# Middle stages of a spectral filter as 64x64 float32 blocks in four quarters of the TensorE array

## Chip, cores and metric

The kernel runs on 1 core of one Trainium2 chip. The metric is the time of one execution on the device in microseconds. Three runs of the kernel before took 3160.31, 3162.1 and 3166.95 us; the median is 3162.1 us.

## What is computed

```python
# x: (8, 3072, 256), filt: (1537, 256) complex
X = rfft(x, axis=1);  y = irfft(X * (filt_r + 1j * filt_i))      # spectral filter
xk = mu_k * y + (1 - mu_k) * y_prev;  xr = mu_r * y + (1 - mu_r) * y_prev   # y_prev: one token back
k = maximum(xk @ w_k, 0);  v = (k * k) @ w_v                     # 256 -> 1024 -> 256
z = sigmoid(xr @ w_r) * v
h = maximum(maximum(z @ w1, z @ w2), z @ w3)                     # 256 -> 768
out = h @ w_out                                                  # 768 -> 256
```

All inputs and outputs are float32.

## The kernel before

A sequence of 3072 tokens is transformed as 96 x 32 points. Stage A works over the 96, and its result goes to DRAM (`s1a`, `s1b`) as 24 groups of four rows for each of 32 residues, 128 rows x 256 channels for a group. Stage B is a 128x128 matrix for each group; its output is multiplied by the complex filter; stage C is another 128x128 matrix for each group, and its result goes to DRAM (`s2`). `y_load` and `y_mm` read it back by chunks of 384 tokens and do the last stage of the inverse transform. B and C are the middle stages. Batch 0 has a transform of its own at the start (`fft_first`). The seven others are done by `fft(b + 1)` beside the dense layers of batch `b`.

In `fft`, B and C go by steps of two groups: 12 steps a batch, 84 in all. Each product is three matmuls in fp32r: high weights by high data, high by low, low by high (`mm3`, L227). So `b_mm` (L489) and `c_mm` (L506) are six matmuls of 128x128 by 256 columns each, into one PSUM bank. For this `split` (L249) makes two parts of the data: a cast on ScalarE (L250) and a subtraction on GpSimd (L251). `b_load` (L476) brings the four weight parts of two groups (512 KB, from a copy in DRAM, `wbc_d`, that twelve GpSimd DMAs make early in the kernel, L1011), the filter (512 KB) and the data (256 KB), and splits the data. After the matmuls of B, three VectorE instructions (L497 to L499) read the bank and multiply by the filter, GpSimd adds (L500), and the sum is split again. After those of C, ScalarE copies the bank (L512) and issues the store.

The order: the dense layers are a list of small units with weights (`units`), the transform of the next batch a list of pieces with weights (`pieces`), and `drive` (L180) mixes them in proportion. A piece of B or C weighs 0.65; an empty piece of 6.0 stands between the first load of B and its first use. That gives the emission order. Each engine's final order is made by a scheduler, which follows a simulated time line and takes of the instructions that are ready the one emitted first, unless it is told another priority. Every matmul waits in TensorE's one queue. All PSUM tiles come from one pool of eight banks under one tag (`ps`, tag `pm`). The SBUF pool `fp` has tags with two or three buffers: `filt`, `fhi`, `flo` and `wbc` three, `fin` and `fo` two. An instruction that needs a buffer waits until the last reader of the buffer's earlier tile is done.

float32 matmuls occur in `fft_first`, in `y_mm` and in `wu_job`; the trace shows each as two records, each with a weight load of its own.

Of the kernel before, what the change touches and what calls it, by code (L numbers as in the profile page):

```python
# [16 lines left out]
N = 3072  # L17
N1 = 48
# [9 lines left out]
GB = NG - GA  # L28
ORDER = [g for g in range(NG) if g % NR == 0] + [g for g in range(NG) if g % NR]


def fft_constants():
# [5 lines left out]
    wi = np.zeros((2, 2, NG, NP))  # L38
    for j in range(2):
        for g in range(NG):  # L40
            ph = 2 * np.pi * ((n1 * g) % N1) / N1
            if g == 0:
                wa[j::2, 0, j, 0] = 1.0
                wa[j::2, 1, j, 0] = (-1.0) ** n1
                wi[0, j, 0, j::2] = 1.0 / N
                wi[1, j, 0, j::2] = (-1.0) ** n1 / N
            else:
                wa[j::2, 0, j, g] = np.cos(ph)
                wa[j::2, 1, j, g] = -np.sin(ph)
                wi[0, j, g, j::2] = 2 * np.cos(ph) / N  # L50
                wi[1, j, g, j::2] = -2 * np.sin(ph) / N
    wb = np.zeros((2, N2, NG, 2, N2))
    wc = np.zeros((2, N2, NG, 2, N2))
    freq = np.zeros((2, N2, NG), np.int64)
    for g in range(NG):
        for s in range(N2):
            if g:
# [8 lines left out]
                wc[0, s, g, 0, :] = c  # L66
                wc[1, s, g, 0, :] = -sg * sn
                wc[0, s, g, 1, :] = sn
                wc[1, s, g, 1, :] = sg * c
                freq[:, s, g] = f if s < NM else N - f  # L70
            else:
# [5 lines left out]
                if s == 0:  # L77
                    wb[0, :, 0, 0, 0] = 1.0
                    wb[0, :, 0, 1, 0] = (-1.0) ** n2
                    wc[0, 0, 0, 0, :] = 1.0  # L80
                    wc[1, 0, 0, 0, :] = (-1.0) ** n2
                    freq[1, 0, 0] = N // 2
                else:
                    wb[src, :, 0, 0, s] = c
                    wb[src, :, 0, 1, s] = -sn
                    wc[0, s, 0, src, :] = 2 * c
                    wc[1, s, 0, src, :] = -2 * sn

    wa, wi, wb, wc, freq = wa[..., ORDER], wi[:, :, ORDER], wb[:, :, ORDER], wc[:, :, ORDER], freq[:, :, ORDER]
    wb = wb.reshape(4, NM, NG, NK).transpose(1, 0, 2, 3)  # L90
    wc = wc.reshape(NK, NG, 4, NM).transpose(0, 1, 3, 2)
    return (
        wa.reshape(NP, NQ),
        wi.reshape(NQ, NP),
        wb.reshape(NK, NG, NK),
        wc.reshape(NK, NG, NK),
# [4 lines left out]
def radix3_constants():  # L101
# [31 lines left out]

    m = np.arange(NM)
    wb = np.zeros((NM, 4, NG, 2, N2))
    for a, g in enumerate(ORDER):
        for s in range(N2):
            if g:
# [8 lines left out]
                wb[:, r + 1, a, 1, s] = sg * cj * c  # L147
            elif s == 0:
                wb[:, 0, a, 0, 0] = 1.0
                wb[:, 0, a, 1, 0] = (-1.0) ** m  # L150
            else:
# [3 lines left out]
                if s < NM:  # L155
                    wb[:, s % 2, a, 0, s] = c
                    wb[:, s % 2, a, 1, s] = -sn
                else:
# [5 lines left out]
    return w3, wb.reshape(NK, NG, NK)  # L164
# [33 lines left out]
def tile_spectral_moe(ctx: ExitStack, tc, x, xr, xz, filt, ones, wa, wa1, wi, wbc, wb1, wc1, filt1, filt0, mu, w_k, w_v, w_r, w1, w2, w3, w_out, out):  # L198
# [25 lines left out]
    def mm(o, wgt, rhs, start, stop, more=False):  # L224
        nc.tensor.matmul(o, lhsT=wgt, rhs=rhs, start=start, stop=stop, skip_group_check=more)  # L225
# [15 lines left out]
    mu_s = cpool.tile([P, 2, 2], F32, name="mu_s")  # L241
    nmu_s = cpool.tile([P, 2, 2], F32, name="nmu_s")
# [839 lines left out]
```

## Time and profile before

| | |
|---|---|
| median of three runs | 3162.1 us |
| profiled execution | 3161.27 us |
| its span, first to last instruction | 3159.5 us |
| TensorE matmuls busy | 3080.0 us, 97%, 19172 records |
| TensorE weight loads busy | 3020.4 us, 96% |
| VectorE / ScalarE / GpSimd busy | 1922.4 / 1884.8 / 1858.6 us (61 / 60 / 59%) |
| mean granted TensorE clock | 0.990 |
| DMA | 705.92 MB, mean 223 GB/s |

A record of a matmul lasts longer than the distance to the next one, since the array is pipelined: the busy time says whether TensorE had a matmul under way, and the distance between two starts says what one costs.

### The profile page before, as it was taken

The page shows a single profiled execution, that of the slowest core. Times are in us where ns is not written, and L with a number is a line of the kernel's source. Part 1 is how long each engine was busy: PE and PEld are TensorE (multiplying, and loading weights), DVE is VectorE, ACT ScalarE, POOL GpSimd, SP SyncE. Part 2 cuts the span into 40 slices and gives each one's busy share as a digit, 9 for nine tenths or more (in the row PEclk, how much of TensorE's full clock was granted, in tenths as well). Part 3 has the DMA queues.
Part 4 walks back from the last instruction along what each step waited for, and adds up shares of the span by engine and source line. Part 5 has one row for each costly group of instructions (what it writes and reads, how often), then busy time and mean ns, then how long its engine had stood idle before and what let it go on. Part 6 is the DMA issues. An engine that isn't in the chain of part 4 may idle for free.

```text
span 3159.5 us, 55818 instructions
## 1 busy us (share of the span) xinstructions
PE 3080.0 (97%) x19172; PEld 3020.4 (96%) x19172; DVE 1922.4 (61%) x3050; ACT 1884.8 (60%) x3968; POOL 1858.6 (59%) x1591
## 2 busy tenths in 40 slices
PE   6799999999999999999999999999999999999998
PEld 4699999999999999999999999999999999999998
DVE  4976676556664666556655566656666566555554
ACT  5556656566565566656666556566666566555554
POOL 3545765567554676556756566556765468444443
PEclk8899999999999999999999999999999999999999
DMA  9878787667776677758767587765887567555554
GB/s 298 267 260 285 235 305 227 188 197 251 260 233 184 224 240 227 254 171 259 251 221 220 183 263 261 227 205 183 262 268 237 180 214 232 178 169 165 161 170 122
DMA packets 400951, 705.92 MB, mean 223 GB/s; under 512 B 41472, under 2 KB 153120, under 8 KB 400032
## 3 DMA queue, kind: packets, MB, share of 16 engines
q1 hardware_dynamic: 333648, 621.26, 62.1%
q10 hardware_dynamic: 64576, 72.45, 6.5%
q0 software_dynamic: 2448, 8.65, 0.8%
q8 instruction: 155, 2.54, 0.3%
q14 instruction: 124, 1.02, 0.1%
HBM read 616.35 MB, written 92.14 MB: 224 GB/s over the span
## 4 chain that ended last, share of the span: by engine, by line
PE 81%; DVE 6%; DMA 5%; POOL 3%; issue 3%; ACT 1%; ACTq 0%; SPq 0%; POOLq 0%; DVEq 0%
PE pb L225 17%; PE pk L225 15%; PE pv L225 14%; PE po L225 12%; PE pe L225 8%; PE pa L225 5%; PE pr L225 4%; PE py L225 3%; DMA ws<-wud 3%; PE pc L225 2%; DVE sc L773 1%; POOL klo L251 1%; DMA s<-e 1%; DVE xd L427 1%; POOL hh L251 1%
## 5 line engine op out<-in xcount | busy, mean ns | idle before, releaser
L225 PE MATMUL pb<-x,ws 128*128 128x384 f32 x3456 | 751.7, 337 | 10.2 <-DMA ws<-wud 7.0
L251 POOL TENSOR_TENSOR hh<-m,hh 128x384 fp32r<-128x384 f32 x384 | 409.5, 1075 | 563.5 <-ACT hh L250 481.4
L251 POOL TENSOR_TENSOR klo<-kr,khi 128x384 fp32r<-128x384 f32 x492 | 520.8, 1064 | 233.2 <-ACT khi L250 205.1
L225 PEld LDWEIGHTS pb<-x,ws 128*128 128x128 f32 x3456 | 596.1, 188 | 20.5 <-issue 6.4
L741 DVE SCALAR_TENSOR_TENSOR kr<-pk,kr 128x384 f32<-128x384 f32 x512 | 281.4, 553 | 429.7 <-ACT kr L740 427.5
L225 PE MATMUL pv<-khi,ws 128*128 128x384 f32 x2048 | 481.3, 338 | 4.9 <-ACT khi L250 4.9
L225 PE MATMUL po<-wo_hi,hh 128*128 128x256 f32 x2304 | 481.4, 282 | 3.3 <-ACT hh L250 2.6
L250 ACT CAST khi<-kr 128x384 fp32r<-128x384 f32 x512 | 261.9, 513 | 226.8 <-DVE kr L741 191.9
L225 PEld LDWEIGHTS po<-wo_hi,hh 128*128 128x128 f32 x2304 | 391.1, 189 | 5.0 <-ACT hh L250 3.4
L225 PE MATMUL pe<-x,ws 128*128 128x384 f32 x1728 | 387.8, 338 | 3.5 <-DVE m L848 1.4
L225 PEld LDWEIGHTS pv<-khi,ws 128*128 128x128 f32 x2048 | 358.9, 188 | 8.5 <-ACT khi L250 6.4
L225 PE MATMUL pk<-xh,wk_hi 128*128 128x384 f32 x1024 | 341.2, 336 | 3.8 <-ACT xh L250 3.8
L225 PE MATMUL pk<-xl,wk_hi 128*128 128x384 f32 x1024 | 343.7, 336 | 0.9 <-DVE xl L251 0.9
L225 PE MATMUL pk<-xh,wk_lo 128*128 128x384 f32 x1024 | 343.3, 335 | 0.0
L225 PE MATMUL po<-wo_lo,hh 128*128 128x256 f32 x1152 | 316.8, 282 | 0.0
L740 ACT ACTIVATE kr<-pk 128x384 f32<-128x384 f32 x512 | 249.8, 489 | 108.8 <-POOL klo L251 56.8
L225 PEld LDWEIGHTS pe<-x,ws 128*128 128x128 f32 x1728 | 297.4, 188 | 8.8 <-DVE sc L855 3.1
L225 PE MATMUL pv<-klo,ws 128*128 128x384 f32 x1024 | 298.6, 338 | 2.4 <-DVE klo L251 1.3
L856 DVE TENSOR_TENSOR m<-sc,m 128x384 f32<-128x384 f32 x384 | 293.9, 768 | 8.4
L251 POOL TENSOR_TENSOR xl<-xm,xh 128x768 fp32r<-128x768 f32 x126 | 234.9, 1880 | 70.3 <-ACT xh L250 70.2
L250 ACT CAST hh<-m 128x384 fp32r<-128x384 f32 x384 | 192.6, 514 | 123.5 <-DVE m L856 85.6
L809 ACT COPY v<-pb 128x384 f32<-128x384 f32 x288 | 138.3, 480 | 188.8 <-PE pb L225 181.4
(134 smaller groups left out, 6143.1 us busy)
## 6 DMA issues: line engine op xcount, KB each, us to landing
ws<-wud SPq DMA_DIRECT2D x864, 256.0 KB, 3.8
ws<-wvd SPq DMA_DIRECT2D x512, 256.0 KB, 3.7
wbc<-wbcd SPq DMA_DIRECT2D x84, 512.0 KB, 5.5
filt<-in_filt SPq DMA_DIRECT2D x84, 512.0 KB, 4.3
ws<-wud SPq DMA_DIRECT2D x288, 128.0 KB, 3.7
xz<-in_xz SPq DMA_DIRECT2D x56, 512.0 KB, 5.2
cin<-s SPq DMA_DIRECT2D x64, 384.0 KB, 4.1
out_dram<-osb ACTq DMA_DIRECT2D x192, 128.0 KB, 2.9
```

Source lines behind the costliest of these rows:

```text
L225: nc.tensor.matmul(o, lhsT=wgt, rhs=rhs, start=start, stop=stop, skip_group_check=more)
L250: nc.scalar.copy(hi, src)
L251: (lo_eng or nc.gpsimd).tensor_tensor(lo, src, hi.bitcast(F32), ALU.subtract)
L427: nc.vector.tensor_tensor(v, z[:, 0], z[:, 1], ALU.subtract)
L740: nc.scalar.activation(r, p, AF.Relu)
L741: nc.vector.scalar_tensor_tensor(r, p, 0.0, r, ALU.max, ALU.mult)
L773: eng.tensor_tensor(t, a, b, ALU.subtract)
L809: nc.scalar.copy(st[to], st[of])
L856: nc.vector.tensor_tensor(m, c, m, ALU.max)
```

## The change

Stages B and C become 64x64 blocks. The frequencies of a group are sorted by parity (`halves_of`), so that each 128x128 matrix of a group is two 64x64 blocks. A step now takes four groups (`NU4` = 6 steps a batch). `quarters` issues eight matmuls of 64x64 by 256 columns in float32: for each pair index `k`, one in each quarter of the array, (rows y, columns x). They go into two PSUM banks, one for each half of the array's rows, and are issued inside `tc.high_priority()`, which gives them the priority of the program's start. There are no parts and no splits of data. The product with the filter is made in each half of 64 partitions: ScalarE copies two blocks of 32 partitions with a sign, VectorE has three instructions, GpSimd multiplies 64 partitions and adds 128. Weights are loaded from the input itself, 256 KB for four groups; the DRAM copy and its twelve GpSimd DMAs go. `s2` has another layout, and `y_load` reads it in two DMAs instead of one. The weights of pieces become 1.1 and 7.7.

```diff
-    def mm(o, wgt, rhs, start, stop, more=False):
-        nc.tensor.matmul(o, lhsT=wgt, rhs=rhs, start=start, stop=stop, skip_group_check=more)
+    def mm(o, wgt, rhs, start, stop, more=False, at=None):
+        nc.tensor.matmul(o, lhsT=wgt, rhs=rhs, start=start, stop=stop, skip_group_check=more, tile_position=at)
...
-    wbc_d = [dp.tile([NK, 4, 2, NK], F32R, tag=f"wbcd{s}", name=f"wbcd{s}", bufs=1) for s in range(NG // 2)]
...
-        s2 = dp.tile([NM, 4, NG, C], F32, tag="s2", name=f"s2_{b}")
+        s2 = dp.tile([2, NM, 2, NG, C], F32, tag="s2", name=f"s2_{b}")
...
+        def quarters(o, of):
+
+            for k in range(2):
+                for y in range(2):
+                    for x in range(2):
+                        w, d = of(y, x, k)
+                        with tc.high_priority():
+                            mm(o[y][x * H : x * H + H, k], w, d, k == 0, True, True, (y * H, x * H))
+
+        def b_load(u):
+            w = fp.tile([NK, 2, 2, 2, H], F32, tag="fhi", name="wbc", bufs=3)
+            nc.sync.dma_start(w, wbc[:, u])
+            f = []
+            sv, g = (s1a, 4 * u) if 4 * u < GA else (s1b, 4 * u - GA)
+            t = fp.tile([NK, 4, C], F32, tag="wbc", name="xb", bufs=3)
+            for y in range(2):
+                d = sv[:, 2 * y : 2 * y + 2, g : g + 4].rearrange("m r g c -> m r (g c)")
+                nc.sync.dma_start(t[y * H : y * H + H], d)
+            for z in range(2):
+                f.append(fp.tile([NK, 2, 2, C], F32, tag="filt", name="filt", bufs=3))
+                nc.sync.dma_start(f[z], filt[:, u, z])
+            st["b", u] = w, f, t
+
+        def b_mm(u):
+            w, f, t = st.pop(("b", u))
+            p = [ps.tile([NK, 2, C], F32, tag="pm", name="pb") for _ in range(2)]
+            quarters(p, lambda y, x, k: (w[y * H : y * H + H, 0, x, k], t[y * H : y * H + H, 2 * x + k]))
+            y = []
+            for z in range(2):
+                fr, fi, q = f[z][:, 0], f[z][:, 1], p[z]
+                v = fp.tile([NK, 2, C], F32, tag="flo", name="v", bufs=3)
+                a, e, m = slice(0, NM), slice(NM, H), NM
+                lo, hi = slice(H, H + NM), slice(H + NM, NK)
+                nc.scalar.mul(v[lo], q[hi], sg_s[hi])
+                nc.scalar.mul(v[hi], q[lo], sg_s[lo])
+                nc.vector.scalar_tensor_tensor(fi[a], q[e], -1.0, fi[a], ALU.mult, ALU.mult)
+                nc.vector.tensor_tensor(fi[e], q[a], fi[e], ALU.mult)
+                nc.vector.tensor_tensor(fr, q, fr, ALU.mult)
+                nc.gpsimd.tensor_tensor(fi[H:], v[H:], fi[H:], ALU.mult)
+                yz = fp.tile([NK, 2, C], F32, tag="fin", name="yz")
+                nc.gpsimd.tensor_tensor(yz, fr, fi, ALU.add)
+                y.append(yz)
+            st["c", u] = w, y
+
+        def c_mm(u):
+            w, t = st.pop(("c", u))
+            p = [ps.tile([NK, 2, C], F32, tag="pm", name="pc") for _ in range(2)]
+            quarters(p, lambda y, x, k: (w[y * H : y * H + H, 1, x, k], t[x][y * H : y * H + H, k]))
+            sv = s2.rearrange("h m r g c -> (h m r) g c")
+            for y in range(2):
+                o = fp.tile([NK, 2, C], F32, tag="fo", name="co")
+                nc.scalar.copy(o, p[y])
+                g = 4 * u + 2 * y
+                nc.scalar.dma_start(sv[:, g : g + 2, :], o)
+
+        for u in range(NU4 + 2):
+            def pb(u=u):
+                if u < NU4:
+                    b_load(u)
+                if 1 <= u <= NU4:
+                    b_mm(u - 1)
+            def pc(u=u):
+                if u >= 2:
+                    c_mm(u - 2)
+            pieces.append((1.1, pb))
+            if u == 0:
+
+                pieces.append((7.7, lambda: None))
+            pieces.append((1.1, pc))
...
-        nc.sync.dma_start(t, s2v[:, q * MC : (q + 1) * MC, :])
+        for h in range(2):
+            nc.sync.dma_start(t[h * 2 * NG : (h + 1) * 2 * NG], s2v[h, :, q * MC : (q + 1) * MC, :])
...
-    for s in range(NG // 2):
-        units.insert(20 + 5 * s, (0.0, lambda s=s: tc.keep_in_program_order(nc.gpsimd.dma_start(wbc_d[s], wbc[:, s]))))
-    n2 = len(wjobs2) + NG // 2
+    n2 = len(wjobs2)
```

The constants of the new layout are made on the host in `radix3_constants` and `quarter_layout`, and so are the input arrays `in_wbc`, `in_filt` and `in_wi`; the shapes of `in_wc1` and of the tensors of `fft_first` stay as they are.

## Rows read from the trace of the kernel before

**Rows 1.** The page: span, then busy us, share of the span and instructions by engine

```profile
span 3159.5 us, 55818 instructions
PE 3080.0 (97%) x19172; PEld 3020.4 (96%) x19172; DVE 1922.4 (61%) x3050; ACT 1884.8 (60%) x3968; POOL 1858.6 (59%) x1591
```

**Rows 2.** The page: chain of work that ended last, shares of the span by engine

```profile
PE 81%; DVE 6%; DMA 5%; POOL 3%; issue 3%; ACT 1%; ACTq 0%; SPq 0%; POOLq 0%; DVEq 0%
```

**Rows 3.** Windows: us, busy us and count per engine, granted clock, DMA share, GB/s

```profile
1240.00:1620.00 380.00, 378.63 (x2384) 374.20 (x2383) 232.99 (x372) 234.55 (x496) 235.84 (x200) 1.00 0.71 228
```

**Rows 4.** Time line of TensorE: start us, us, instruction; a set of B, then of C

```profile
741.54 0.28 PE L225 MATMUL pb<-xbh,wbc 128*128 128x256 f32 x1
741.66 0.28 PE L225 MATMUL pb<-xbl,wbc 128*128 128x256 f32 x1
...
742.26 0.34 PE L225 MATMUL pb<-x,ws 128*128 128x384 f32 x1
...
1507.78 0.28 PE L225 MATMUL pc<-yh,wbc 128*128 128x256 f32 x1
...
1508.48 0.28 PE L225 MATMUL po<-wo_hi,hh 128*128 128x256 f32 x1
```

**Rows 5.** Groups by line and form: count, busy us, mean ns, idle before and releasers

```profile
L225 PE MATMUL pc<-yh,wbc 128*128 128x256 f32 x336 | 75.7, 283 | 2.2 <-DVE m L848 1.4 <-DVE filt L499 0.7
L225 PE MATMUL pb<-xbh,wbc 128*128 128x256 f32 x336 | 75.7, 281 | 0.5 <-issue 0.5
```

**Rows 6.** Time line of TensorE: float32 matmuls of 256 columns in the first transform

```profile
83.70 0.59 PE L225 MATMUL pc<-q,wci 128*128 128x256 f32 x2
84.13 0.59 PE L225 MATMUL pc<-filt,wcr 128*128 128x256 f32 x2
84.56 0.60 PE L225 MATMUL pc<-q,wci 128*128 128x256 f32 x2
```

**Rows 7.** Windows: the same stretch, with its granted clock

```profile
83.60:84.80 1.20, 1.20 (x8) 1.05 (x7) 0.19 (x1) 0.74 (x2) 0.94 (x1) 1.00 0.00 0
```

**Rows 8.** Time line of TensorE: float32 matmuls of 96 columns

```profile
2743.83 0.61 PE L225 MATMUL py<-wi_s,cin 96*128 96x96 f32 x4
2744.28 0.39 PE L225 MATMUL py<-wi_s,cprev 96*128 96x96 f32 x2
```

**Rows 9.** Time line of TensorE: another set of B, with the instructions within it

```profile
656.12 0.40 PE L225 MATMUL pb<-xbh,wbc 128*128 128x256 f32 x2
656.36 0.28 PE L225 MATMUL po<-wo_hi,hh 128*128 128x256 f32 x1
...
656.83 0.28 PE L225 MATMUL pb<-xbl,wbc 128*128 128x256 f32 x1
```

**Rows 10.** Time line of SyncE's queue: loads of stage B's data, batch 2

```profile
580.13 0.81 SPq L483 DMA_DIRECT2D xb<-s1a  x2
```

**Rows 11.** The instructions on the filter tile, 500 to 860 us: ns min/median/max, first and last start

```profile
L497 DVE SCALAR_TENSOR_TENSOR filt<-pb,filt x12: 692/693/695, 657.3 to 816.5; 64x512 f32<-64x512 f32 x12
L499 DVE TENSOR_TENSOR filt<-pb,filt x12: 691/692/693, 658.7 to 817.9; 128x512 f32<-128x512 f32 x12
```

**Rows 12.** Groups by line and form: the other engines' work on stages B and C

```profile
L251 POOL TENSOR_TENSOR yl<-filt,yh 128x512 fp32r<-128x512 f32 x84 | 115.2, 1371 | 19.6 <-ACT yh L250 18.7 <-PE pb L225 0.8
L500 POOL TENSOR_TENSOR filt<-filt 128x512 f32<-128x512 f32 x84 | 109.6, 1305 | 127.9 <-DVE filt L499 120.1 <-PE pv L225 3.5 <-PE pe L225 2.6
L250 ACT CAST yh<-filt 128x512 fp32r<-128x512 f32 x84 | 52.1, 621 | 17.0 <-POOL filt L500 16.9
L512 ACT COPY co<-pc 128x512 f32<-128x512 f32 x84 | 49.2, 585 | 35.3 <-PE pc L225 35.1
L650 ACT COPY v<-pb 64x512 f32<-64x512 f32 x12 | 7.0, 582 | 15.2 <-PE pb L225 12.3 <-POOL wf L294 2.3 <-ACT e L582 0.5
```

**Rows 13.** DMA issues: count, KB each, median us to landing

```profile
wbc<-wbcd SPq DMA_DIRECT2D x84, 512.0 KB, 5.5
filt<-in_filt SPq DMA_DIRECT2D x84, 512.0 KB, 4.3
cin<-s SPq DMA_DIRECT2D x64, 384.0 KB, 4.1
```

More of the change, by code (lines that the diff above doesn't have):

```diff
@@ L132, in radix3_constants @@
     w3 = np.stack([wa0.reshape(NK, NK), wa12.reshape(NK, NK)], axis=1)
+    p = np.arange(NP)
+    wf = np.zeros((4, NG, NP))
+    for a, g in enumerate(ORDER):
+        for r, f in ((0, g), (2, N1 - g)) if g else ((2, NG),):
+            ph = 2 * np.pi * (f * p % NP) / NP
+            wf[r, a] = 2 * np.cos(ph) / N
+            wf[r + 1, a] = -2 * np.sin(ph) / N
+        if not g:
+            wf[0, a] = 1.0 / N
+            wf[1, a] = (-1.0) ** p / N
     m = np.arange(NM)
     wb = np.zeros((NM, 4, NG, 2, N2))
+    wc = np.zeros((2, N2, NG, NM, 4))
     for a, g in enumerate(ORDER):
@@ L163, in radix3_constants, with halves_of, quarter_layout @@
                     wb[:, 3, a, 1, s] = cj * c
-    return w3, wb.reshape(NK, NG, NK)
+                    wc[0, s, a, :, 2] = c
+                    wc[1, s, a, :, 2] = -sn
+                    wc[0, s, a, :, 3] = cj * sn
+                    wc[1, s, a, :, 3] = cj * c
+    return w3, wb, wc, wf.reshape(NQ, NP)
+def halves_of(a):
+    s = np.arange(N2)
+    return (s[s % 2 == 0], s[s % 2 == 1]) if ORDER[a] else (s[:NM], s[NM:])
+def quarter_layout(wb, wc, filt_r, filt_i, freq):
+    C = filt_r.shape[1]
+    w = np.zeros((NU4, 2, 2, 2, 2, H, H))
+    f = np.zeros((NU4, 2, 2, H, 2, 2, C), filt_r.dtype)
+    fq = freq.reshape(2, N2, NG)
+    for u in range(NU4):
+        for x in range(2):
+            for k in range(2):
+                a = 4 * u + 2 * x + k
+                for z, s in enumerate(halves_of(a)):
+                    w[u, 0, x, k, z] = wb[:, 2 * z : 2 * z + 2, a][..., s].reshape(H, H)
+                    w[u, 1, x, k, z] = wc[:, s, a, :, 2 * z : 2 * z + 2].reshape(H, H)
+                    f[u, z, x, :, 0, k] = filt_r[fq[:, s, a]].reshape(H, C)
+                    f[u, z, x, :, 1, k] = filt_i[fq[:, s, a]].reshape(H, C)
+                    if ORDER[a] == 0 and z == 0:
+                        f[u, z, x, 0, 1, k] = 0.0
+                        f[u, z, x, NM, 1, k] = 0.0
+    wq = np.zeros((2, H, NU4, 2, 2, 2, H), np.float32)
+    wq[:, :, :, 0] = w[:, 0].transpose(3, 4, 0, 1, 2, 5)
+    wq[:, :, :, 1] = w[:, 1].transpose(1, 4, 0, 3, 2, 5)
+    f = f.transpose(2, 3, 0, 1, 4, 5, 6)
+    return wq.reshape(NK, NU4, 2, 2, 2, H), f.reshape(NK, NU4, 2, 2, 2, C)
 def as_float(bits):
@@ L241, in tile_spectral_moe @@
     mu_s = cpool.tile([P, 2, 2], F32, name="mu_s")
+    sg_s = cpool.tile([NK, 1], F32, name="sg_s")
+    for k in range(NK // NM):
+        nc.gpsimd.memset(sg_s[k * NM : (k + 1) * NM], 1.0 - 2.0 * (k % 2))
     nmu_s = cpool.tile([P, 2, 2], F32, name="nmu_s")
@@ L690, in y_load @@
             e = mp.tile([NQ, C], F32, tag="cprev", name="cprev", bufs=1)
-            nc.sync.dma_start(e, s2v[:, NM - 1, :])
+            for h in range(2):
+                nc.sync.dma_start(e[h * 2 * NG : (h + 1) * 2 * NG], s2v[h, :, NM - 1, :])
         cs["c", i] = t, e
```

99 lines of the change are left out of this document (20 added, 79 removed).

## The prediction

> **What bounds the kernel now.** I read the page's busy shares first: TensorE has a matmul under way for 97% of the span, the other three engines work 59 to 61% of it [rows 1]. The chain of work that ended last agrees: 81% of it is TensorE, no other engine has over 6% [rows 2]. Then the windows, to see whether a middle stretch leaves anything open: from 1240 to 1620 us, one whole batch, TensorE is busy for 378.63 of 380 us at the full granted clock [rows 3]. So in the steady part there is no idle time in which a longer middle stage could hide, and none that a shorter one could leave unused by itself: what the change gives or takes in TensorE's queue goes into the span one to one, and the other engines count only if TensorE comes to wait for them.
>
> The size of what is replaced comes from the time line. A set of six matmuls takes 741.54 to 742.26, 0.72 us, in stage B, and 1507.78 to 1508.48, 0.70 us, in stage C [rows 4]; a start every 0.118 us, while one record lasts 0.28 us. There are 336 + 336 records with the high data [rows 5], four in a set, so 168 sets, and at 0.71 us they are 119 us of the span. That is all the change can win on.
>
> **The change part by part.**
>
> *Matmuls.* Two old sets, 1.42 us, become one group of eight float32 matmuls; 12 groups a batch, 84 in all. A float32 matmul of 256 columns at full clock [rows 7] costs 0.43 us: the pairs of records start at 83.70, 84.13 and 84.56 [rows 6], so 0.215 us a record. Eight of them are 16 records. What no row shows is how matmuls in four quarters share the time. Bounds: one after another, 16 x 0.215 = 3.44 us; four at a time, 4 x 0.215 = 0.86 us. I take four at a time, since nothing ties the quarters together: each has its own 64 partitions of data, its own weights, and the two halves of rows write different banks. It is the nearest in kind to what the trace has, where a record begins 0.12 us after the one before while that one still runs for 0.16 us [rows 4].
>
> *Going in and out.* A group sits between matmuls of the whole array. If the array must be empty on both sides, each costs the part of a record that is now overlapped: 0.28 - 0.12 = 0.16 us, 0.32 us a group; lower bound nothing. I take the whole. The rule that speaks against this change is in the Trainium skill, TensorEngine Tiling (Array Packing), section Tiling Modes: a change of the tiling mode drains TensorE. No row here has such a change; by the rule the 0.32 us are paid, and without it the group would be 0.32 us shorter.
>
> *Weights.* Sixteen weight loads of 64 columns replace twelve of 128. The price of 128 shows where the columns are few: four float32 records of 96 columns start within 0.45 us [rows 8], 0.112 us each, more than the 0.08 us that their 96 columns would take at the 0.215 us for 256. Half of that, 0.056 us, is my estimate for 64. Only the first of a group stands open if the rest load beside other quarters' matmuls. One group is then 0.86 + 0.32 + 0.06 = 1.24 us, and it saves 1.42 - 1.24 = 0.18 us; times 84: 15 us.
>
> *Order.* Today a set may be split at no cost: one of B has other matmuls within it, from 656.36 to 656.83 [rows 9]. A split group would drain twice more, and the priority is there against that. But a bank is still given in emission order from one pool, so a group can't run far ahead of its place. It runs when its two banks come free, ahead of dense matmuls that are ready. Its data are long there: in batch 2 the first loads are issued at 580.13 [rows 10] and the first product with the filter begins at 657.3 [rows 11]. What is late next is a bank: a group at the head of the queue waits for the reader of the bank's last tile, and all of the dense work stands behind it, since TensorE has one queue. The trace bounds this: at present 1.4 + 0.7 us of waiting stand before 168 sets [rows 5], about 0.02 us each; above, a whole copy of a bank, 0.585 us [rows 12], at each of 84 groups, 49 us. I take 0.05 us, near the lower row: 4 us.
>
> *Reading the banks.* For two steps ScalarE had two casts of the data, two of the sum and two copies, all near 0.6 us: 3.7 us; now four signed copies and two copies. Fewer partitions are no cheaper (64 partitions took 582 ns, 128 took 585 [rows 12]), so 3.5 us. VectorE keeps six instructions of 0.69 us. GpSimd had six operations of 1.3 to 1.4 us, 8 us, and keeps four, 5.3 us: 42 x 2.7 = 113 us less in all. All of it lies beside TensorE's work and is worth nothing by itself. The cover is the distance of steps: an old step comes each (816.5 - 657.3) / 11 = 14.5 us [rows 11], a new one thus about 25 us, with some 8 us of VectorE and ScalarE work between.
>
> *Transfers.* The weights go from 84 x 512 KB to 42 x 256 KB [rows 13]; the early copy in DRAM and its twelve issues go. SyncE has 42 issues fewer for B and 64 + 8 more for `y_load`, at 0.4 us or less of its queue each [rows 10]: nothing, as long as the dense weights come early. One wait is new: with three `filt` buffers and two per step, the second filter load of a step waits for GpSimd's first add of the step before, and that waits for a `fin` buffer, which the earlier group of C must release. From there 2 x 1.3 us of GpSimd and 4.3 us of landing [rows 12, 13], 7 us, against a distance of pieces of some 12 us. VectorE's queue would stand behind a late load; I price it at nothing, and at 84 x 0.5 = 42 us if the cover were gone.
>
> **The sum.** 3161.3 us for the profiled execution, less 15, plus 4: 3150 us. The median of runs was 0.8 us above the profiled one: 3151 us.
>
> **The rivals.**
>
> *Two at a time.* The two records of one float32 matmul need the same quarter, so the second waits for the first; if TensorE starts matmuls strictly in order, the next quarter's first record stands behind it and only two quarters ever work together. Nine steps of 0.215 us are 1.94 us, with both drains and the first load 2.32 us: 84 x 0.90 = 75 us more, 3238 us with the 0.8; with the drains hidden 2.0 us, 49 us more, 3211 us. For it speaks that the two records of a pair stand next to each other [rows 6] and that all starts in the time line are in order [rows 4]; against it nothing but that the trace has no quarters. It decides from 1.42 us a group. The Trainium skill, TensorE: Matmul & The Clock Gate, Part 3, says that matmuls start and end in program order, which is this rival's ground; it also says that tiles start some 4 ns apart, which is the forecast's, for tiles with one matmul each. No row settles it.
>
> *Weight loads one after another.* Sixteen at 0.056 us are 0.90 us, and the last quarter's last record can only start after its own: some 1.27 us, 1.59 with the drains. 84 x 0.17 = 14 us more, plus the 4: 3180 us. For it: 96-column records go at the pace of their weights [rows 8].
>
> *Broken groups* (the change doesn't do what it says). If banks come one by one, dense matmuls fill in between the halves of a group, and each break costs another 0.32 us. One break a group is 27 us: 3178 us; it turns the sign from 0.4 breaks a group. For it: sets are broken today [rows 9].
>
> *Drains that cost nothing.* 0.92 us a group, 42 us less, plus 4: 3124 us.
>
> *One after another.* 3.44 + 0.38 = 3.82 us, 202 us more: 3364 us.
>
> **How the numbers follow.** Forecast (1.24 us) 0.38, with a range of its own of 3138 to 3158; two at a time 0.20; serial weights 0.15; broken groups 0.12; free drains 0.10; serial 0.05. What can be told from no change here is 0.2%, 6.3 us. Faster: nearly all of the forecast, the free drains and a little of the broken groups, 0.46. Same: the forecast's upper end and the mild cases of serial weights and broken groups, 0.12. Slower: the rest, 0.42. The predicted time is the likeliest case's, 3151 us. The range holds all but the slower half of two at a time, the serial case and the lowest of the free drains: 3122 to 3225 us.
>
> **What would show it.** In the time line of TensorE, four matmuls of 64x64 starting within some hundredths of a microsecond, and 1.1 to 1.3 us from a group's first start to the next dense matmul's: the forecast; 2 us or more: two at a time, with starts 0.2 us apart; 1.5 to 1.6 us with starts 0.06 us apart: the weights. Dense matmuls inside a group show breaks. Idle time before `pb` and `pc` that ends with ScalarE or VectorE shows waits for banks; waits of VectorE for `filt` show the filter loads. GpSimd should be some 110 us less busy and DMA move some 40 MB less. I am wrong if the group is over 1.42 us, or if waits before groups come to over 0.2 us each.

## The result, and the profile after

The changed kernel takes 3199.32 us in the median of four runs (3197.85 to 3202.59), the kernel before 3161.2 us in the runs beside it: a ratio of 1.0119 [1.0101, 1.0136], so it is slower by 38 us. The forecast was 3151 us, 10 us faster than before; 3199 us lies inside the stated range of 3122 to 3225 us, but the change went the other way. The profiled spans are 3200.7 and 3159.5 us, 41.2 us apart.

The page of the changed kernel: span, busy us by engine, and the shares of the chain that ended last.

```profile
span 3200.7 us, 56204 instructions
...
PE 3119.8 (97%) x19508; PEld 2966.4 (93%) x19508; DVE 1889.7 (59%) x3050; ACT 1924.2 (60%) x3968; POOL 1740.4 (54%) x1499
...
DMA packets 388953, 666.64 MB, mean 208 GB/s; under 512 B 41760, under 2 KB 153408, under 8 KB 388032
...
PE 86%; DVE 6%; DMA 3%; ACT 2%; issue 2%; POOL 1%; SPq 0%; ACTq 0%; POOLq 0%; DVEq 0%
```

Beside [rows 1, 2]: GpSimd works 118 us less (about 110 were expected), DMA moves 39 MB less (some 40), and TensorE is still at 97%. Its share of the chain rose from 81 to 86%. The middle of the span looks almost as full as in [rows 3]; the windows' columns are us, busy us and count of TensorE, its weight loads, VectorE, ScalarE and GpSimd, granted clock, DMA share, GB/s:

```profile
1240.00:1620.00 380.00, 376.72 (x2391) 358.84 (x2391) 224.53 (x363) 234.72 (x485) 213.97 (x185) 1.00 0.68 210
```

So the time is in TensorE's queue, and what it holds is seen in the time line. One group of the changed kernel that runs whole (start us, us from the first start to the last end, instruction, records):

```profile
1526.59 0.69 PE L264 MATMUL pe<-x,ws 128*128 128x384 f32 x3
1527.21 1.11 PE L264 MATMUL pb<-xb,wbc 64*64 64x256 f32 x16
1528.24 0.38 PE L264 MATMUL po<-wo_hi,hh 128*128 128x256 f32 x1
1528.47 0.28 PE L264 MATMUL po<-wo_lo,hh 128*128 128x256 f32 x1
```

From 1527.21 to 1528.24 is 1.03 us for all 16 records, a little below the 1.1 to 1.3 us that the forecast named as its sign. But another group, 24 us earlier, runs in two halves:

```profile
1502.00 0.68 PE L264 MATMUL pa<-x,ws 128*128 128x384 f32 x3
1502.61 1.08 PE L264 MATMUL pb<-xb,wbc 64*64 64x256 f32 x8
1503.62 0.50 PE L264 MATMUL po<-wo_hi,hh 128*128 128x256 f32 x2
1503.96 0.68 PE L264 MATMUL pb<-x,ws 128*128 128x384 f32 x3
1504.48 0.68 PE L264 MATMUL pe<-x,ws 128*128 128x384 f32 x3
1505.00 0.69 PE L264 MATMUL pb<-x,ws 128*128 128x384 f32 x3
1505.62 1.08 PE L264 MATMUL pb<-xb,wbc 64*64 64x256 f32 x8
1506.63 0.57 PE L264 MATMUL py<-wi_s,cin 96*128 96x96 f32 x3
```

Eight records, half the work, take 1.01 us each time, 1502.61 to 1503.62 and 1505.62 to 1506.63: as long as sixteen. A half is the four matmuls of one bank, which is one half of the rows and so two quarters; each quarter still has its two matmuls of two records, 4 x 0.215 us, while the other two quarters stand empty. Of the 84 groups 42 run whole and 42 in two halves, with 3 to 31 dense records between the halves.

**The account.** To see what this is worth I added up, over all of TensorE's records after 110 us, the distance from each start to the next. Distances that touch a 64x64 record are the groups, less the usual pace of the dense record before them. What the first dense record behind a group takes over its pace is added, so that going in and out is within, and so is a wait in front of a group. In the kernel before, the middle stages are their 1008 records at 0.118 us. For all other dense records, whatever is over the usual pace of their form (0.174 us for 384 columns, 0.118 for 256, and so on) is called a wait. What is left, the dense work at its pace and the first 110 us, is 2978 to 2981 us in all twenty traces. That it is so alike follows from the way of counting, since the dense work is the same in all; it means that a difference between two spans is the difference of the two columns.

Not all of what is called a wait is waiting: the records that start while the granted clock is at the lower of its two levels (0.5, 1.2 GHz) hold 6.1 us of it in the kernel before, 11.4 us in the changed one, and 4 to 21 us in the twenty traces.

| trace | span | middle stages | waits |
|---|---|---|---|
| before | 3159.5 | 118.9 | 60.3 |
| after | 3200.7 | 156.7 | 64.6 |

The middle stages cost 37.8 us more and the waits 4.3 us more: 42.1 of 41.2 us. The 118.9 agrees with the 119 of the prediction. A whole group costs 1.237 us (from the kernel of the first experiment below, where all 84 are whole: 103.9 / 84). With whole groups the forecast's saving is there: 118.9 - 103.9 = 15.0 us. In the changed kernel the 84 halves cost 101.1 us, each 1.18 to 1.22 us and 1.203 in the mean, so a break costs 2 x 1.203 - 1.237 = 1.17 us, and 42 breaks 49 us. One whole group, at 409.96 us, takes 4.96 us, 3.7 more than usual: TensorE waits 0.46 us before it and 1.46 us within it for a bank, and its rest runs at the lower clock (0.53 from 412 to 419 us). So the 37.8 us are -15.0 + 49.1 + 3.7.

Before the groups themselves TensorE hardly waits. Groups of the changed kernel by line and form (count, busy us, mean ns, idle before and its releasers):

```profile
L264 PE MATMUL pc<-yz,wbc 64*64 64x256 f32 x672 | 70.1, 393 | 1.9 <-DVE filt L552 1.9
L264 PE MATMUL pb<-xb,wbc 64*64 64x256 f32 x672 | 68.6, 389 | 0.0
...
L553 POOL TENSOR_TENSOR filt<-v,filt 64x512 f32<-64x512 f32 x84 | 108.2, 1289 | 121.2 <-issue 46.4 <-DMA ws<-wud 39.3 <-ACT v L549 23.4
...
L550 DVE SCALAR_TENSOR_TENSOR filt<-pb,filt 32x512 f32<-32x512 f32 x84 | 57.3, 682 | 64.7 <-ACT v L549 56.9 <-DMA filt<-in_filt 3.0 <-issue 2.0
L548 ACT ACTIVATE v<-pb,sg_s 32x512 f32<-32x512 f32 x84 | 57.3, 682 | 38.8 <-PE pb L264 37.9
```

The 1.9 us are the two waits of that one group, as little as in [rows 5]. They end with L552, VectorE's last read of the two banks of the group of B at 399.93 us; the group's own data, the sums `yz`, were there at 399.3. VectorE waited once for a filter load, 3.0 us. ScalarE's signed copy of 32 partitions takes 0.68 us, more than the 0.585 of the plain copy [rows 12].

### The profile page after: what moved, and what is told of

The parts are those of the page before. It is cut to its first block, busy times and chain, and to the rows that moved or that the text cites. A ratio compares the mean times of both kernels' runs of the same rounds, so it can differ in the third digit from the quotient of the medians.

```text
span 3200.7 us, 56204 instructions
## 1 busy us (share of the span) xinstructions
PE 3119.8 (97%) x19508; PEld 2966.4 (93%) x19508; DVE 1889.7 (59%) x3050; ACT 1924.2 (60%) x3968; POOL 1740.4 (54%) x1499
## 3 DMA queue, kind: packets, MB, share of 16 engines
q14 instruction: 123, 1.01, 0.1%
## 4 chain that ended last, share of the span: by engine, by line
PE 86%; DVE 6%; DMA 3%; ACT 2%; issue 2%; POOL 1%; SPq 0%; ACTq 0%; POOLq 0%; DVEq 0%
PE pb L264 20%; PE pk L264 13%; PE pv L264 13%; PE po L264 13%; PE pe L264 9%; PE pa L264 6%; PE pr L264 4%; PE py L264 4%; PE pc L264 2%; DVE sc L829 1%; DVE x L293 1%; PE ps L264 1%; DMA ws<-wud 1%; DVE kr L797 1%; POOL klo L293 1%
## 5 line engine op out<-in xcount | busy, mean ns | idle before, releaser
L264 PE MATMUL pv<-khi,ws 128*128 128x384 f32 x2048 | 487.9, 340 | 13.5 <-ACT khi L292 13.4
L264 PE MATMUL po<-wo_hi,hh 128*128 128x256 f32 x2304 | 489.3, 284 | 2.7 <-ACT hh L292 2.0
L264 PE MATMUL pv<-klo,ws 128*128 128x384 f32 x1024 | 305.5, 341 | 6.9 <-POOL klo L293 6.0
```

## The experiments

Every kernel is named by its label; those named held have e1's edit, and their diffs show only what is changed beside it. The scheduler makes the order of the instructions anew for each kernel. The table holds the median of its runs, its ratio to the kernel before on the same chip with the interval, and its account (us, profiled execution).

| label | median | ratio | span | middle | waits |
|---|---|---|---|---|---|
| e1_held | 3183.71 | 1.0068 [1.0053, 1.0083] | 3183.5 | 103.9 | 100.2 |
| e2_first_at_turn | 3193.02 | 1.0094 [1.0077, 1.0111] | 3194.4 | 132.3 | 83.3 |
| e3_no_priority | 3249.97 | 1.0278 [1.0263, 1.0293] | 3248.0 | 178.4 | 90.6 |
| e4_own_banks | 3263.48 | 1.0318 [1.0303, 1.0334] | 3263.6 | 126.5 | 157.2 |
| e5_held_twice | 3238.22 | 1.024 [1.0225, 1.0256] | 3236.8 | 178.9 | 78.4 |
| e6_held_no_v | 3157.98 | 0.9983 [0.9974, 0.9993] | 3156.6 | 104.0 | 73.6 |
| e7_held_dve | 3220.41 | 1.0186 [1.0169, 1.0203] | 3218.0 | 105.2 | 134.0 |
| e8_held_rows | 3194.51 | 1.0104 [1.0089, 1.0119] | 3191.2 | 106.7 | 105.3 |
| e9_held_lag4 | 3205.12 | 1.0134 [1.0119, 1.015] | 3205.0 | 103.7 | 120.6 |
| e10_before_lag4 | 3166.06 | 1.0012 [1.0003, 1.0022] | 3162.3 | 118.9 | 63.2 |
| e11_changed_no_v | 3209.6 | 1.0144 [1.0127, 1.0161] | 3210.0 | 167.5 | 62.7 |
| e12_held_mix | 3191.1 | 1.0092 [1.0077, 1.0107] | 3189.4 | 106.2 | 104.5 |
| e13_before_two_thirds | 3156.13 | 0.9981 [0.9972, 0.999] | 3158.0 | 79.3 | 99.4 |
| e14_before_touch | 3175.61 | 1.005 [1.0033, 1.0066] | 3168.5 | 118.9 | 70.2 |
| e15_held_no_priority | 3199.66 | 1.0122 [1.0107, 1.0137] | 3197.5 | 120.0 | 99.1 |
| e16_held_weights | 3205.46 | 1.0139 [1.0122, 1.0156] | 3201.8 | 106.5 | 116.4 |
| e17_before_weights | 3196.6 | 1.0108 [1.0093, 1.0123] | 3196.1 | 118.9 | 97.2 |
| e18_two_thirds_weights | 3173.5 | 1.0038 [1.0023, 1.0053] | 3174.0 | 79.3 | 115.3 |

### Are the broken groups the cost?

**e1_held**: VectorE touches both banks before the group, so that no matmul of it can start until both are granted, and the eight matmuls keep their order on TensorE with nothing between them.

```diff
+            nc.vector.memset(o[1][:, 0, :1], 0.0)
+            nc.vector.tensor_copy(o[0][:, 0, :1], o[1][:, 0, :1])
+            with tc.manual_schedule(engines={mybir.EngineType.PE}):
...
```

> Every group of eight quarter matmuls kept whole: VectorE touches one column of both banks first, so the first half cannot start before the second bank is free. Theory 1 (split groups): the changed kernel has 42 whole groups at about 1.24 us and 84 halves at about 1.2 us, 153 us; 84 whole groups are 104 us, so 49 us less: about 3150 us, some 11 us under the kernel before. Theory 2 (the groups are cheap enough, and the dense work behind them waits, for banks and for the engines that read them): splitting does not matter, about 3190 to 3200 us.

All 84 groups are whole, and the middle stages cost 103.9 us instead of 156.7: the 52.8 us were in the breaks (49) and in the one long group (4). But the time falls by 16 us only, since the waits of the dense work rise from 64.6 to 100.2. The first half of the theory is shown; that the kernel then gets the 52.8 us is refuted. The same rows by form, and the same window, in this kernel:

```profile
L264 PE MATMUL pb<-xb,wbc 64*64 64x256 f32 x672 | 46.0, 389 | 1.2 <-DVE pb L518 1.2
...
L264 PE MATMUL pc<-yz,wbc 64*64 64x256 f32 x672 | 46.0, 389 | 0.0
```

```profile
1240.00:1620.00 380.00, 373.63 (x2402) 357.60 (x2401) 230.09 (x391) 234.59 (x488) 217.31 (x186) 1.00 0.69 214
```

The busy time of the records fell by 46.7 us (138.7 to 92.0), the wait for the new touches is 1.2 us, and gaps have opened in the steady window: 6.37 us without any matmul against 3.28 in the changed kernel and 1.37 in [rows 3]. Records overlap, so this shows only the longer waits.

**e2_first_at_turn**: the eight matmuls in fixed order, the first of a group without priority, the other seven with it.

```diff
+            with tc.manual_schedule(engines={mybir.EngineType.PE}):
...
+                    with tc.high_priority() if n > 0 else ExitStack():
...
```

> Fixed order inside a group, its first matmul at its own turn, the other seven with priority. 52 groups stay whole, 32 become two matmuls and then six. Theory 1: 52 x 1.24 + 32 x (0.8 + 1.24) = 130 us against 153, about 3176 us. Theory 2: about 3190 to 3200 us, as the banks come as before.

52 groups run whole, 32 as two matmuls and six. The kernel stands about half way between the changed one and e1, in the middle stages (132.3) and in the waits (83.3). Fewer breaks alone don't give a time below the kernel before.

**e3_no_priority**: the changed kernel without the priority.

```diff
-                        with tc.high_priority():
-                            mm(o[y][x * H : x * H + H, k], w, d, k == 0, True, True, (y * H, x * H))
+                        mm(o[y][x * H : x * H + H, k], w, d, k == 0, True, True, (y * H, x * H))
```

> The changed kernel without the priority. The groups come in 162 runs instead of 126, 25 of them whole. Theory 1: about 184 us of runs against 153, about 3230 us. Theory 2: nothing jumps ahead of ready dense matmuls any more, so fewer waits, about 3180 us or less.

The groups fall into 162 runs, 25 whole, and the time rises by 50 us over the changed kernel: 22 us in the middle stages, 26 us in the waits. So the priority does act against breaks, as the prediction said; it can't act before the second bank is there.

**e4_own_banks**: six banks for the dense work, and one tile of two banks for the groups.

```diff
-    ps = ctx.enter_context(tc.tile_pool(name="ps", bufs=8, space=bass.MemoryType.PSUM))
+    ps = ctx.enter_context(tc.tile_pool(name="ps", bufs=6, space=bass.MemoryType.PSUM))
+    pq = ctx.enter_context(tc.tile_pool(name="pq", bufs=1, space=bass.MemoryType.PSUM))
...
```

> A PSUM pool of its own for the groups, one tile of two banks; six banks left for the dense work. 70 groups whole, 14 in two runs. Theory 1: 70 x 1.24 + 14 x 2.05 = 115 us against 153, about 3162 us if six banks do for the dense work. Theory 2: the dense work has fewer banks and waits longer, over 3200 us.

70 groups run whole, and the middle stages cost 126.5 us; but the waits are 157.2 us. Waits of TensorE by what it waited for (us, times, longest):

```profile
PE pb L265 <- ACT pa L873: 10.3, 25, 0.5
PE po L265 <- POOL hh L294: 8.0, 7, 1.2
PE pa L265 <- DMA ws<-wud: 7.6, 6, 2.6
PE pb L265 <- ACT u L868: 5.7, 9, 3.0
...
PE pe L265 <- DVE m L911: 5.2, 7, 1.3
```

The first and the fourth are dense products that are added onto a bank which ScalarE must copy first (6.6 and 0.5 us in e1). The last is a new dense tile that waits until VectorE has read a bank, 5.2 us, a wait that e1 has not, as one expects with six banks for the dense work instead of eight. These lines are a part of the 157 us; for the rest the cause is not shown. Banks of their own, two of the eight, are no way out here.

### How long is a group, and in which order do its matmuls start?

**e5_held_twice**: each group's eight matmuls issued twice.

```diff
-                for n in range(8):
+                for n in (*range(8), *range(8)):
```

> Whole groups as in e1_held (3183.7 us), and each group's eight matmuls issued twice, back to back. Four quarters at a time: 84 x 4 x 0.215 = 72 us more, about 3256 us, and the price of a group is then 0.86 us of passes and the rest going in and out. Two at a time: 144 us more. If the waits of the dense work are lasting, they shrink a little, since TensorE has more to do meanwhile: 3240 to 3256 us.

```profile
1491.01 0.68 PE L264 MATMUL pb<-x,ws 128*128 128x384 f32 x3
1491.62 1.96 PE L264 MATMUL pb<-xb,wbc 64*64 64x256 f32 x32
1493.51 1.31 PE L264 MATMUL pb<-x,ws 128*128 128x384 f32 x6
```

This is 1.89 us from the first start to the next dense one against 1.03: eight more matmuls cost 0.86 us in this group, which is the four passes of the forecast (0.89 us in the mean of all 84). In one group of e1, at 1184.37 us, the records start in fours 6 to 7 ns apart, at 0, 7, 13, 20, and the next four at 267, 273, 280, 287 ns; in this group of e5 the starts are the same within 1 ns. In the whole kernel the middle stages take 75.0 us more than in e1, and the time is 54.5 us longer: the waits fell by 22 us, so the exchange that ate e1's gain is seen in this direction too.

**e8_held_rows**: the four matmuls of one row half emitted ahead of the other four.

```diff
-                    k, y, x = n // 4, n // 2 % 2, n % 2
+                    y, k, x = n // 4, n // 2 % 2, n % 2
```

> Whole groups as in e1_held, but the four matmuls of the first half of the rows ahead of the four of the second half. If TensorE starts matmuls strictly in order, the second half starts when the first has little left, 1.72 us instead of 0.86 us of passes: about 72 us more, 3256 us. If it lets a later matmul of a free quarter pass an earlier one that waits for its quarter: no change, 3184 us.

```profile
1517.54 0.69 PE L264 MATMUL pe<-x,ws 128*128 128x384 f32 x3
1518.15 1.11 PE L264 MATMUL pb<-xb,wbc 64*64 64x256 f32 x16
1519.19 0.44 PE L264 MATMUL pk<-xh,wk_hi 128*128 128x384 f32 x1
```

The group takes 1.04 us again, and the first eight starts are at 0, 7, 27, 34, 267, 274, 294 and 300 ns. The second row half begins 27 ns after the first, although two matmuls that must wait for their quarters until 0.48 us stand ahead of it; the two records that signal the end of a bank are the second of each pair, so the pairs are the row halves. In strict order the second half would have begun at 0.48 us and the group taken about as much longer, some 40 us in all (a little over half of what was expected for that case). The changed kernel's own whole group at 1527.21 has these starts too: 0, 7, 27, 33 ns. The order within a group is not the cost. Of the 7.7 us between its span and e1's, 2.8 lie in the middle stages and 5.1 in the waits.

### Where do the 36 us of waits come from?

The first idea was the short bursts of the other engines. In e1_held four signed copies of ScalarE come together (time lines of ScalarE, then of TensorE):

```profile
1185.50 0.68 ACT L550 ACTIVATE v<-pb,sg_s 32x512 f32<-32x512 f32 x1 [0.50 <-PE pb L264]
...
1187.60 0.68 ACT L551 ACTIVATE v<-pb,sg_s 32x512 f32<-32x512 f32 x1
1188.30 0.48 ACT L867 COPY v<-pb 128x384 f32<-128x384 f32 x1
```

```profile
1187.07 0.68 PE L264 MATMUL pa<-x,ws 128*128 128x384 f32 x3
1188.83 3.23 PE L264 MATMUL pb<-x,ws 128*128 128x384 f32 x15 [1.08 <-ACT v L867]
```

The copy of a dense bank at 1188.30, which must be done before the next product is added onto that bank, stands behind them, and TensorE waits 1.08 us for it. In this kernel seven waits ended by that line come to 7.0 us. A place like this is a cause of its own wait; whether it explains the 36 us is another question.

**e6_held_no_v**: e1 without the signed copies and GpSimd's product; it leaves out the imaginary part of the product with the filter on the upper 64 partitions.

```diff
...
-                nc.scalar.mul(v[lo], q[hi], sg_s[hi])
-                nc.scalar.mul(v[hi], q[lo], sg_s[lo])
...
-                nc.gpsimd.tensor_tensor(fi[H:], v[H:], fi[H:], ALU.mult)
```

> Whole groups as in e1_held, without ScalarE's four signed copies per step and GpSimd's two products of 64 partitions (this leaves out the imaginary part of the product with the filter on the upper 64 partitions). Theory 3 (bursts: the work of two banks at once on ScalarE and GpSimd makes the squares of the dense layer late, for which TensorE waits): the waits before pv and pb fall by some 25 us, about 3158 us. Theory 2b (the wait is for banks given in pairs, or comes from the order alone): about 3180 us.

The waits fall by 26.6 us to 73.6, with whole groups. This spoke for the bursts, and the next runs test it.

**e7_held_dve**: the upper half's product on VectorE.

```diff
...
-                nc.scalar.mul(v[lo], q[hi], sg_s[hi])
-                nc.scalar.mul(v[hi], q[lo], sg_s[lo])
+                nc.vector.scalar_tensor_tensor(fi[lo], q[hi], -1.0, fi[lo], ALU.mult, ALU.mult)
+                nc.vector.tensor_tensor(fi[hi], q[lo], fi[hi], ALU.mult)
...
-                nc.gpsimd.tensor_tensor(fi[H:], v[H:], fi[H:], ALU.mult)
```

> Whole groups as in e1_held, the product on the upper 64 partitions made by VectorE as on the lower ones: ScalarE loses 168 copies of 0.68 us, GpSimd 168 half products become none, VectorE gets four instructions of 0.68 us more per step. Theory 3: about 3165 to 3172 us, if VectorE has room (59% busy). If the time for which the two banks are held is what counts: over 3184 us, as one engine now reads both.

ScalarE and GpSimd are free of the bursts, and yet the waits are 134.0 us. VectorE now has five instructions for a bank instead of three, and TensorE waits 10.7 us before `pe` for one VectorE instruction on `m` (never in e1): that fits dense VectorE work that stands behind them, but it is a part of the rise only. Some 15 us of the rise are records at the lower clock (21.1 against 5.6 in e1).

**e12_held_mix**: this for the second bank of a group only.

```diff
+                if z == 0:
+                    nc.scalar.mul(v[lo], q[hi], sg_s[hi])
+                    nc.scalar.mul(v[hi], q[lo], sg_s[lo])
+                else:
+                    nc.vector.scalar_tensor_tensor(fi[lo], q[hi], -1.0, fi[lo], ALU.mult, ALU.mult)
+                    nc.vector.tensor_tensor(fi[hi], q[lo], fi[hi], ALU.mult)
...
```

> Whole groups as in e1_held; the upper half of the first bank by ScalarE and GpSimd, that of the second bank by VectorE. Theory 3: the burst on ScalarE is half as long, 1.4 us instead of 2.7, VectorE's grows from 4.1 to 5.5 us; e7 says that VectorE has no room, so between 3175 and 3205 us.

The waits are 104.5 us, no better than in e1.

**e11_changed_no_v**: the edit of e6 in the changed kernel, where groups break; it leaves out the same.

```diff
...
-                nc.scalar.mul(v[lo], q[hi], sg_s[hi])
-                nc.scalar.mul(v[hi], q[lo], sg_s[lo])
...
-                nc.gpsimd.tensor_tensor(fi[H:], v[H:], fi[H:], ALU.mult)
```

> The changed kernel with its split groups (31 whole, 106 halves by its order), without ScalarE's signed copies and GpSimd's half products (this leaves out the imaginary part of the product with the filter on the upper 64 partitions). If splits and bursts add up: 3199 + 11 (more halves) - 26 = about 3184 us. If the splits matter only through the bursts: about 3160 us.

The waits are 62.7 us against 64.6: the same instructions that seemed to be worth 26 us in e6 are worth 2 here, and the time rises, since more groups break (31 whole; middle stages 167.5). Bursts as the general cause are not borne out.

**e9_held_lag4** and **e10_before_lag4**: the dense layers get one more unit of distance between a product and its use (and one weight buffer less, for room), in e1 and in the kernel before.

```diff
-    LAG = 3
+    LAG = 4
...
-    ws = ctx.enter_context(tc.tile_pool(name="ws", bufs=10))
+    ws = ctx.enter_context(tc.tile_pool(name="ws", bufs=9))
```

> Whole groups as in e1_held, and the second matrix of the dense layer lags four blocks behind the first instead of three (one dense weight buffer fewer, nine, to make room). Theory 3 (bursts make the squares late): a block of slack, about 1 us, covers most waits before pv; some 20 us less, about 3164 us. If the waits come from banks or from the order: about 3184 us.

> The kernel before with the same lag of four and nine weight buffers: the control for e9_held_lag4. Its waits before pv are some 10 us longer than the pace asks for, so 3150 to 3160 us by theory 3; no change by the other.

More slack in the dense chain should have covered delays of the other engines. In e1 it adds 20.4 us of waits; in the kernel before it changes them by 2.9. One buffer less costs nothing there, so the loss in e9 isn't plainly that.

**e14_before_touch**: a touch of VectorE before each set of the kernel before.

```diff
+            nc.vector.memset(p[:, 0, :1], 0.0)
```

(and the same in `c_mm`.)

> The kernel before, with VectorE setting one column of the bank before each set of B and C, as the whole groups of e1_held have it: 168 short instructions, each waiting in VectorE's queue for the bank to be free. If this is what makes the dense work wait in e1_held: 3180 us or more. If not: 3160 to 3166 us.

The waits are 9.9 us longer with 168 touches. e1 has as many, so by this measure the touches explain some 10 of its 36 us.

**e15_held_no_priority**: e1 without the priority.

```diff
-                    with tc.high_priority():
-                        mm(o[y][x * H : x * H + H, k], w, d, k == 0, True, True, (y * H, x * H))
+                    mm(o[y][x * H : x * H + H, k], w, d, k == 0, True, True, (y * H, x * H))
```

> Groups held and ordered as in e1_held, without the priority: 71 whole, the others in two or three runs, about 119 us of groups against 104. If the 40 us of added waits in e1_held come from the groups that go ahead of dense matmuls: the waits fall and the time is about 3160 to 3165 us. If they come from the work of two banks at once, or from the hold: about 3195 us.

The waits are 99.1 us, as in e1: they are there without groups that go ahead of dense matmuls. Without priority 71 groups are whole and the middle stages cost 16 us more.

### Does any gain on TensorE arrive? Does the order alone move the time?

**e13_before_two_thirds**: the kernel before, with four of the six matmuls of a set and no other edit; it leaves out the product of low weights and high data.

```diff
-                mm3(p[:, g], [(w[:, 0, g], w[:, 1, g])], [(hi[:, g], lo[:, g])], g > 0, True)
+                mm(p[:, g], w[:, 0, g], hi[:, g], g == 0, False, True)
+                mm(p[:, g], w[:, 0, g], lo[:, g], False, True, True)
```

(and the same in `c_mm`.)

> The kernel before with four of the six matmuls of each set of B and C (the product of low weights and high data is left out, so the result is less exact), all else as it was. 336 matmuls fewer at 0.118 us are 40 us of TensorE. Theory 4a (the dense work can use any time that the middle stages free): about 3122 us. Theory 4b (the other engines are so near their own limit that freed time comes back as waits, whatever the form of the middle stages): 3140 us or more.

39.6 us of matmuls are gone from TensorE's queue, and the time falls by 6 us: the waits rise by 39.1. No new instruction, no touch and no break is in this kernel. But the order of the rest is not the same either: of the 18164 other records of TensorE, 15318 have the same tiles at the same place as in the kernel before, so the 39.1 us are not shown to come from the removal alone. Waits of TensorE in it:

```profile
PE pe L225 <- DVE m L850: 15.8, 12, 3.8
...
PE pb L225 <- DMA ws<-wud: 8.5, 10, 1.4
PE pv L225 <- ACT khi L250: 8.5, 12, 1.8
PE pa L225 <- DMA ws<-wud: 5.8, 6, 1.7
```

Several different engines end them, none with more than 16 us: the dense layers' VectorE chain, the loads of their weights, and ScalarE's cast (4.9 us in the kernel before).

**e17_before_weights** and **e18_two_thirds_weights**: only the weights of pieces changed, in the kernel before and in e13 (first diff); **e16_held_weights**: likewise in e1 (second diff).

```diff
-            pieces.append((0.65, pb))
+            pieces.append((0.55, pb))
...
-                pieces.append((6.0, lambda: None))
+                pieces.append((7.7, lambda: None))
...
-            pieces.append((0.65, pc))
+            pieces.append((0.55, pc))
```

```diff
-            pieces.append((1.1, pb))
+            pieces.append((1.3, pb))
...
-                pieces.append((7.7, lambda: None))
+                pieces.append((6.0, lambda: None))
...
-            pieces.append((1.1, pc))
+            pieces.append((1.3, pc))
```

> The kernel before with weights 0.55 and 7.7 for 0.65 and 6.0: the control. If its 60 us of waits are an accident of a well-placed order: 3175 us or more. If not: 3160 to 3170 us.

> e13_before_two_thirds (the product of low weights and high data left out) with weights 0.55 and 7.7. If the return of only 6 of the 40 us was an accident of the order: 3140 us or less. If freed time comes back as waits in any order: 3150 to 3162 us.

> Whole groups as in e1_held, with other weights of the pieces (1.3 and 6.0 for 1.1 and 7.7), which only shift where the steps stand among the dense work. If the 100 us of waits in e1_held are an accident of the order: they move by 20 us or more, and the time with them (3184 +- 20 us). If the freed time cannot be used by the dense work: 3178 to 3190 us.

The order alone moves the kernel before by 34 us: with the same instructions the waits go from 60.3 to 97.2, about as much as all of e1's increase. In e1 another order gives 16 us more of waits and 22 us more of time. Waits of TensorE in e17_before_weights:

```profile
PE pb L225 <- DMA ws<-wud: 17.7, 12, 3.1
...
PE pb L225 <- ACT pa L814: 9.0, 7, 1.5
PE pv L225 <- ACT khi L250: 6.2, 9, 1.8
```

The loads of dense weights in the first line stood for 7.0 us in the kernel before. And from e17 to e18 the same 39.6 us of matmuls are worth 23 us, not 6. So the kernel before stands at the low end of what its order can give (60; 63 and 70 in e10 and e14), and what a gain on TensorE brings depends on where the order leaves the waits.

## Why the prediction was wrong, point by point

- **The step that failed** is in *Order* and in the rival *Broken groups*: "the priority is there against that", and "each break costs another 0.32 us". Half of the groups break, 42 of 84, and a break costs 1.17 us. The prediction priced a break by the two drains alone; a half of a group works in two quarters only and needs its 0.86 us again. 0.86 + 0.32 from the prediction's own numbers are 1.18 us. With this price the rival gives 42 x 1.18 = 50 us over the forecast, 3201 us, against 3199 measured; it had the chance 0.12, and its sign turns from (15 - 4) / 84 / 1.18 = 0.11 breaks a group, not from 0.4. The prediction's own sign of being wrong is met, a group over 1.42 us: 156.7 / 84 = 1.87.
- **Why they break** was named rightly (banks come one by one from one pool): holding the group until both banks are there makes all 84 whole (e1). The priority acts against breaks, 22 us of the middle stages in e3, but sends the first half off as soon as its own bank comes.
- **The price of a whole group** was right: 1.24 us forecast, 1.237 measured, and with it the saving of 15 us (118.9 - 103.9). Four at a time is shown by the starts of records in fours and by the 0.86 us of a second group (e5). *Two at a time* (starts 0.2 us apart), *weight loads one after another* (starts 0.06 us apart) and *one after another* (3.8 us) fall. *Drains that cost nothing* falls too: in e1 the last dense record before a group takes 0.09 us more than its pace, the next dense start comes 0.09 us later than a pass after the last record's, and the dense record after that takes 0.10 us more, 0.28 us beside the 0.32. The Trainium skill, TensorEngine Tiling (Array Packing), section Tiling Modes, has the drain at a change of mode; the trace agrees and gives it this price. The first pass takes 0.267 us, the later ones 0.216; the 0.05 us between them are close to the 0.06 us for the first weight load.
- **Waits for banks**: 4 us were predicted, 0.05 us at each group. One group of 84 waits so, 1.9 us, and with the lower clock behind it it costs 3.7 us: the size was right, by a single group. The 4.3 us by which the waits of the dense work grew are something else, and the part of them at the lower clock alone grew by 5.3 us. The upper bound of 49 us was far off. (The lower row was also misread: 1.4 + 0.7 us before 168 sets are 0.0125 us each, not 0.02; nothing hangs on it.)
- **Reading the banks, transfers, GpSimd, the filter loads**: nothing of the loss is there, as priced; the filter loads held VectorE for 3.0 us. The signed copy was 0.68 instead of 0.585 us.
- **"What the change gives or takes in TensorE's queue goes into the span one to one"** is wrong for what it gives. It held for the loss of this change (37.8 and 41.2 us), but 52.8 us less from after to e1 brought 16, and 39.6 us less in e13 brought 6, 23 in another order (e18). The order of the other instructions changed with each of these, so what a gain brings in an unchanged order is not shown. And busy time hid waits: in the kernel before, TensorE's gaps after 110 us come to 30 us, and the distances between starts show 60. So the breaks are not all that stood between the change and a gain: e1, with every group whole and with its touches, is still slower than the kernel before by 0.68%.

**What stays open**: which part of the waits that came with each gain is lasting, and what sets it. Without the priority they are as long (99.1 us), the touches explain some 10 us, and the bursts of ScalarE and GpSimd were worth 26 us in one order and 2 in another; the order changed in each of these runs as well. The three lowest sums of middle stages and waits are alike, 179.2 (before), 178.7 (e13) and 177.6 us (e6), which would fit a second chain just under the present time; no run shows such a chain, and the 37 us that the order alone makes are as large as what is to be explained. None of the whole-computation kernels tried was faster than the kernel before.

## What to carry to other kernels

Price a piece that runs in parallel parts as its longest part: half of it can take as long as the whole, so ask what may come between the parts, and let it start only when everything it writes into has been granted. A queue that looks 97% busy need not pass a gain on; take the distance between starts against the usual pace to see the waits in it, and remove matmuls (as in e13) to see what a gain brings before building on it. A scheduler that makes the order anew changes more than the edit, so change the order alone once (as in e17): if that moves the time by more than the expected gain, the gain can't be read from a single order.

## What the runs showed of the hardware that was not expected

A matmul for a free quarter starts ahead of an earlier one that waits for its own: in e8 the second row half began 27 ns after the first, with two waiting matmuls emitted ahead of it, and the group took 1.04 us, against 1.03 in the whole group above. The Trainium skill, TensorE: Matmul & The Clock Gate, Part 3, has matmuls start and end in program order, with tiles some 4 ns apart; the 6 to 7 ns here are near the second, and e8 differs from the first, so here the measurement decides.

The weight loads of a 64x64 block show 129 to 133 ns each in e8, sixteen of them within a group of 1.04 us, and didn't set the pace. ScalarE's copy with a factor for each partition took 0.68 us for 32 partitions, longer than the plain copy of 128.
